# The last output tile in two column halves, each with its own bank, output tile, engine and queue

One core of one Trainium2 chip. The metric is the device time of one execution in microseconds (us), median of several. All runs told here are fast, with a granted TensorE clock of 0.997 to 1.0. The experiments ran in batches on several chips, each beside the kernel before.

In the views PE is TensorE, DVE VectorE, ACT ScalarE and SP SyncE; a q behind the name is the engine's queue. PSUM is the memory into which TensorE writes its sums, in banks. A semaphore is a counter that instructions wait for. A transfer's landing is its arrival; the profile gives the time from issue to landing. Of each view only the lines that matter are shown, and code and diffs are shortened.

## The reference

Linformer attention over 8 batches and 8 heads, then a dense layer with a hard-swish. The change touches only the last product, `g @ w_out`, and of its 64 output tiles of 128 tokens by 512 columns only the last.

```python
k_proj = einsum('ks,bhsd->bhkd', E, k); v_proj = einsum('ks,bhsd->bhkd', F, v)
attn = softmax(q @ k_proj^T / sqrt(64)); x = (attn @ v_proj) as [8192 tokens, 512]
h = x @ w_in                       # [8192, 2048]
g = h * clip(h + 3, 0, 6) / 6
out = g @ w_out                    # [8192, 512], float32
```

## The kernel before

The order of instructions on each engine is the order of the program. `pmm()` gives a bank of PSUM (128 x 512 float32) from a ring of four, `opool` an output tile from a ring of four. For the last tile the program already had a branch: two half copies on two engines and two transfers on two queues, but one bank and one output tile.

```python
opool = ctx.enter_context(tc.tile_pool(name="o", bufs=4))
ps_mm = ctx.enter_context(tc.tile_pool(name="ps_mm", bufs=4, space=bass.MemoryType.PSUM))
def pmm():
    return ps_mm.tile([P, TOK], f32, tag="mm", name="mm")
# ... cut ...
def second_group(b, t, g, c, copy=None):
    o_ps = pmm()
    for fo in range(FO):                      # 16 matmuls of 512 columns
        nc.tensor.matmul(o_ps, g[:, fo, c * P:(c + 1) * P], w_out_sb[:, fo, :],
                         start=(fo == 0), stop=(fo == FO - 1))
        if fo % SB == SB - 1:
            yield
    o_sb = opool.tile([P, d_model], f32, tag="o_sb", name="o_sb")
    o_dst = out_rows(b, t, c)
    if (b, t, c) == (B - 1, NB - 1, SB - 1):
        half = slice(0, d_model // 2), slice(d_model // 2, d_model)
        nc.vector.tensor_copy(o_sb[:, half[0]], o_ps[:, half[0]])
        nc.scalar.copy(o_sb[:, half[1]], o_ps[:, half[1]])
        nc.sync.dma_start(out=o_dst[:, half[0]], in_=o_sb[:, half[0]])
        nc.scalar.dma_start(out=o_dst[:, half[1]], in_=o_sb[:, half[1]])
        return
    (copy or nc.scalar.copy)(o_sb, o_ps)
    nc.sync.dma_start(out=o_dst, in_=o_sb)
# ... cut ...
for c in range(SB):                           # the last four tiles, nothing beside them
    whole(second_group(*behind[0], c))
```

The softmax here doesn't subtract the row's maximum and nothing guards it: scores larger than these inputs give would overflow.

## Time and profile before

| | before |
|---|---|
| median of the first 3 runs | 511.65 us (511.52 to 511.9) |
| span of the profiled run, which took 511.81 us | 510.0 us |
| TensorE busy | 98% |
| last matmul ends, by the chain | 505.91 us |
| last transfer issued | 506.85 us |

The page gives each engine's busy time and the chain of work that ended last; the timeline gives start, length, engine, line and what ended the idle time before it. TensorE bounds the body. The change concerns the 4.1 us between its last matmul and the end. This is the closing line of the program, L613, on SP's queue in the stretch of the tail: count, lengths in ns, first and last start.

```profile
L613 SPq EVENT_SEMAPHORE  x11: 17/28/28, 506.8 to 510.0; - x11
L613 SPq DRAIN  x3: 7/7/13, 509.2 to 509.5; - x3
```

SP waits for semaphores one after another, drains for the first time at 509.2, and the closing barrier runs to 510.0. The last transfer landed at about 506.85 + 1.8 = 508.65, so some 0.55 us lie between that and the first drain.

### The profile page before, as it was taken

The page shows a single profiled execution, that of the slowest core. Times are in us where ns is not written, and L with a number is a line of the kernel's source. Part 1 is how long each engine was busy: PE and PEld are TensorE (multiplying, and loading weights), DVE is VectorE, ACT ScalarE, POOL GpSimd, SP SyncE. Part 2 cuts the span into 40 slices and gives each one's busy share as a digit, 9 for nine tenths or more (in the row PEclk, how much of TensorE's full clock was granted, in tenths as well). Part 3 has the DMA queues.
Part 4 walks back from the last instruction along what each step waited for, and adds up shares of the span by engine and source line. Part 5 has one row for each costly group of instructions (what it writes and reads, how often), then busy time and mean ns, then how long its engine had stood idle before and what let it go on. Part 6 is the DMA issues. An engine that isn't in the chain of part 4 may idle for free.

```text
span 510.0 us, 7106 instructions
## 1 busy us (share of the span) xinstructions
PE 497.4 (98%) x2750; PEld 224.3 (44%) x2802; DVE 257.5 (50%) x401; ACT 274.5 (54%) x493; POOL 37.9 (7%) x57
## 2 busy tenths in 40 slices
PE   8899999999899999999999999999999999999996
PEld 3444444444344444444444444444444444444442
DVE  3572735855655733656434743467444563334420
ACT  3657476567576545664466644674447654444431
POOL 8610020010100200002000020000000000000000
PEclk9999999999999999999999999999999999999999
DMA  9999999599299493516924188421110111101112
GB/s 165 199 205 207 202 156 236 97 159 176 88 184 186 91 218 76 125 41 91 225 57 94 52 141 169 107 58 33 42 41 25 38 42 42 42 21 42 41 51 74
DMA packets 74210, 55.39 MB, mean 109 GB/s; under 512 B 35520, under 2 KB 65984, under 8 KB 74176
## 3 DMA queue, kind: packets, MB, share of 16 engines
q0 software_dynamic: 31952, 29.36, 37.0%
q1 hardware_dynamic: 42000, 25.17, 19.4%
q10 hardware_dynamic: 224, 0.39, 0.3%
q8 instruction: 22, 0.36, 0.3%
q14 instruction: 12, 0.10, 0.1%
HBM read 59.24 MB, written 16.78 MB: 149 GB/s over the span
## 4 chain that ended last, share of the span: by engine, by line
PE 94%; DMA 3%; issue 1%; POOL 1%; DVE 0%; ACT 0%; DVEq 0%; POOLq 0%
PE mm L470 43%; PE mm L450 43%; PE at L181 3%; DMA w_in_sb<-in_moe_w_in_dram 2%; PE at L227 1%; PE mm L227 1%; DMA k<-in_k_dram 1%; PE at L209 1%; PE mm L209 0%; PE at L370 0%; POOL q L97 0%; DVE kp L187 0%; POOL k L101 0%; PE at L350 0%; DVE xT L246 0%
## 5 line engine op out<-in xcount | busy, mean ns | idle before, releaser
L456 DVE SCALAR_TENSOR_TENSOR g<-r,mm 128x512 bf16<-128x512 f32 x256 | 173.8, 686 | 131.8 <-ACT r L455 130.4
L470 PE MATMUL mm<-w_out_sb,g 128*128 128x512 bf16 x995 | 231.8, 379 | 1.7 <-issue 0.5
L450 PE MATMUL mm<-xT,w_in_sb 128*128 128x512 bf16 x1001 | 229.2, 379 | 3.1 <-DVE xT L246 1.2
L455 ACT ACTIVATE r<-mm 128x512 f32<-128x512 f32 x256 | 152.8, 599 | 76.2 <-PE mm L450 73.7
L450 PEld LDWEIGHTS <-w_in_sb 128*128 128x128 bf16 x1024 | 99.4, 98 | 124.0 <-issue 5.5
L470 PEld LDWEIGHTS <-g 128*128 128x128 bf16 x1024 | 98.0, 98 | 121.5 <-issue 7.2
L484 ACT COPY o_sb<-mm 128x512 f32<-128x512 f32 x35 | 20.3, 587 | 91.5 <-PE mm L470 91.5
L484 DVE COPY o_sb<-mm 128x512 f32<-128x512 f32 x28 | 19.3, 691 | 67.3 <-PE mm L470 64.2
L159 ACT ACTIVATE rec<-mm 128x512 f32<-128x512 f32 x34 | 19.0, 595 | 34.1 <-PE mm L227 17.6
L163 ACT ACTIVATE rec<-rec 128x512 f32<-128x512 f32 x60 | 35.6, 637 | 0.0
L246 DVE TENSOR_TENSOR xT<-at,rec 128x512 bf16<-128x512 f32 x44 | 28.1, 680 | 7.1 <-ACT rec L163 7.1
L218 ACT ACTIVATE aT<-at 128x512 bf16<-128x512 f32 x44 | 23.1, 613 | 0.9 <-PE at L209 0.9
L159 ACT ACTIVATE rec<-at 128x512 f32<-128x512 f32 x30 | 17.3, 598 | 6.0 <-PE at L227 3.7
L199 POOL COPY mark<-kT 1x1 bf16<-1x1 bf16 x5 | 0.9, 178 | 210.1 <-DMA kT<-kp 210.1
L181 PE MATMUL at<-k,e_t 128*64 128x512 bf16 x56 | 13.4, 382 | 0.0
L181 PE MATMUL at<-v,f_t 128*64 128x512 bf16 x56 | 13.4, 382 | 0.0
L187 DVE CAST kp<-at 64x512 bf16<-64x512 f32 x14 | 9.0, 678 | 4.9 <-PE at L181 4.9
L218 ACT ACTIVATE aT<-mm 128x512 bf16<-128x512 f32 x12 | 6.5, 594 | 8.9 <-PE mm L209 8.9
L190 DVE CAST vp<-at 64x512 bf16<-64x512 f32 x14 | 9.7, 694 | 0.4
L181 PEld LDWEIGHTS <-e_t 128*64 128x64 bf16 x56 | 5.6, 109 | 7.2 <-PE at L227 2.1
L479 DVE COPY o_sb<-mm 128x256 f32<-128x256 f32 x1 | 0.4, 425 | 16.0 <-PE mm L470 16.0
L227 PE MATMUL at<-aT,vp 64*64 64x512 bf16 x88 | 8.5, 376 | 0.0
(62 smaller groups left out, 147.0 us busy)
## 6 DMA issues: line engine op xcount, KB each, us to landing
out_dram<-o_sb SPq DMA_DIRECT2D x63, 256.0 KB, 2.0
k<-in_k_dram POOLq DMA_DIRECT2D x7, 1024.0 KB, 15.4
v<-in_v_dram POOLq DMA_DIRECT2D x7, 1024.0 KB, 21.0
q<-in_q_dram POOLq DMA_DIRECT2D x7, 1024.0 KB, 10.5
w_out_sb<-in_moe_w_out_dram POOLq DMA_DIRECT2D x4, 512.0 KB, 17.1
k<-in_k_dram POOLq DMA_DIRECT2D x4, 256.0 KB, 5.8
v<-in_v_dram POOLq DMA_DIRECT2D x4, 256.0 KB, 7.9
w_in_sb<-in_moe_w_in_dram POOLq DMA_DIRECT2D x2, 512.0 KB, 11.9
```

The costliest lines, as they stand in the source:

```text
L159: nc.scalar.activation(ln, den, AF.Ln)
L163: nc.scalar.activation(ln, ln, AF.Exp, scale=-1.0)
L181: nc.tensor.matmul(ps[e * KP:(e + 1) * KP], ef_t[e][:, so, :], kqv[self.b]["kv"[e]][:, :, so, :], start=(so == 0), stop=(so == SO - 1))
L190: nc.vector.tensor_copy(self.vp[a * KP:(a + 1) * KP], self.ps[KP:].rearrange("p (h d) -> p h d", d=D))
L218: nc.scalar.activation(self.aT[j][:, r].rearrange("p a n -> p (a n)"), tiles[r], AF.Exp, scale=scale)
L227: nc.tensor.matmul(tiles[t][c:c + D].rearrange("p (r n) -> p r n", r=2), stationary(r, 2 * j + a), self.aT[j][r:r + KP, :, a, :], start=Tr ...
L246: nc.vector.tensor_mul(self.xT[:, j, t, :], av[t], recs[t])
L450: nc.tensor.matmul(h_ps, w_in_sb[:, ko, fo * P:(fo + 1) * P], xT[:, ko, t, :], start=(ko == 0), stop=(ko == KO - 1))
L455: nc.scalar.activation(r, h_ps, AF.Relu, bias=0.5, scale=1.0 / 6.0)
L456: nc.vector.scalar_tensor_tensor(g[:, fo, :], r, 1.0, h_ps, op0=ALU.min, op1=ALU.mult)
L470: nc.tensor.matmul(o_ps, g[:, fo, c * P:(c + 1) * P], w_out_sb[:, fo, :], start=(fo == 0), stop=(fo == FO - 1))
L484: (copy or nc.scalar.copy)(o_sb, o_ps)
```

## The change

The intent: the left half finishes while TensorE still works on the right one, and its copy and transfer are gone from behind the last matmul.

```diff
 def second_group(b, t, g, c, copy=None):
+    o_dst = out_rows(b, t, c)
+    if (b, t, c) == (B - 1, NB - 1, SB - 1):
+        for e, copy, dma in ((0, nc.vector.tensor_copy, nc.sync), (1, nc.scalar.copy, nc.scalar)):
+            half = slice(e * d_model // 2, (e + 1) * d_model // 2)
+            o_ps = pmm()[:, :d_model // 2]
+            for fo in range(FO):
+                nc.tensor.matmul(o_ps, g[:, fo, c * P:(c + 1) * P], w_out_sb[:, fo, half],
+                                 start=(fo == 0), stop=(fo == FO - 1))
+            o_sb = opool.tile([P, d_model], f32, tag="o_sb", name="o_sb")[:, :d_model // 2]
+            copy(o_sb, o_ps)
+            dma.dma_start(out=o_dst[:, half], in_=o_sb)
+        return
     o_ps = pmm()
     # ... 16 matmuls of 512 columns, unchanged ...
-    if (b, t, c) == (B - 1, NB - 1, SB - 1):
-        ... two half copies out of one bank, two transfers ...
-        return
```

More of the change, by code (lines that the diff above doesn't have):

```diff
@@ L474, in second_group @@
         o_sb = opool.tile([P, d_model], f32, tag="o_sb", name="o_sb")
-        o_dst = out_rows(b, t, c)
-        if (b, t, c) == (B - 1, NB - 1, SB - 1):
-            half = slice(0, d_model // 2), slice(d_model // 2, d_model)
-            nc.vector.tensor_copy(o_sb[:, half[0]], o_ps[:, half[0]])
-            nc.scalar.copy(o_sb[:, half[1]], o_ps[:, half[1]])
-            nc.sync.dma_start(out=o_dst[:, half[0]], in_=o_sb[:, half[0]])
-            nc.scalar.dma_start(out=o_dst[:, half[1]], in_=o_sb[:, half[1]])
-            return
         (copy or nc.scalar.copy)(o_sb, o_ps)
```

## The prediction

> **What bounds the kernel now.** I read the page first, by engine and by line, to see what sets the length of the whole.
>
> ```profile
> PE 497.4 (98%) x2750; PEld 224.3 (44%) x2802; DVE 257.5 (50%) x401; ACT 274.5 (54%) x493; POOL 37.9 (7%) x57
> PE 94%; DMA 3%; issue 1%; POOL 1%; DVE 0%; ACT 0%; DVEq 0%; POOLq 0%
> L470 PE MATMUL mm<-w_out_sb,g 128*128 128x512 bf16 x995 | 231.8, 379 | 1.7 <-issue 0.5
> ```
>
> TensorE is busy in 98% of the span and holds 94% of the chain that ended last; line 470, the second product, is one of its two large groups. The change does not touch that body. It touches the last of 64 output tiles, so the question is what stands behind the last matmul. For that I read the chain of waits over the last 20 us and then the timeline of the last seven, in order of time (start, length, what).
>
> ```profile
> 497.10 8.81 PE mm L470 x40
> 505.91 0.04 DVEq L479
> 505.94 0.04 issue
> 505.98 0.44 DVE o_sb L479
> 506.42 0.02 issue
> 506.44 0.37 ACT o_sb L480
> ```
>
> ```profile
> 502.52 0.59 ACT L484 COPY o_sb<-mm 128x512 f32<-128x512 f32 x1 [2.91 <-PE mm L470]
> ...
> 505.98 0.42 DVE L479 COPY o_sb<-mm 128x256 f32<-128x256 f32 x1 [16.00 <-PE mm L470]
> 506.44 0.33 SPq L481 DMA_DIRECT2D out_dram<-o_sb  x1
> 506.44 0.37 ACT L480 COPY o_sb<-mm 128x256 f32<-128x256 f32 x1 [3.34 <-DVE o_sb L479]
> 506.85 0.36 ACTq L482 DMA_DIRECT2D out_dram<-o_sb  x1
> ```
>
> The reader is to see two things. The two half copies were written to run side by side, on two engines, but they run one after the other: ScalarE's copy is released by VectorE's ("<-DVE o_sb L479"), not by TensorE, because both read one bank. And the last transfer is issued at 506.85, 0.94 us after the last matmul ended at 505.91. What follows is fixed: that transfer lands 1.8 us after its issue (the page of DMA issues in the window), at about 508.65, the SP queue's own waits show it waiting 1.9 us for it, and the closing semaphores run to 510.0, another 1.35 us. The sum 505.91 + 0.94 + 1.8 + 1.35 is the span of 510.0; 511.65 is the measured time, 1.65 us more for a start and end that the span leaves out, and which I take as unchanged.
>
> **What the Trainium skill says.** (1) "PSUM — Partial Sum Buffer", section "PSUM bank collisions raise a hardware error": no two engines may access one bank in the same partitions at once, two reads of disjoint columns included, and a dependency has to keep them apart. The trace agrees: the 0.46 us from 505.98 to 506.44 are that dependency. Two banks need none. (2) "TensorE: Matmul & The Clock Gate", section "Back-to-back issue gap": N columns take N / 2.4 + 2.5 ns in a stream, but with a weight load to each matmul 128 columns sustain only some 81 ns. The trace agrees with the first and not with the second, worked out below (56 ns with loads). (3) "DMA: Bandwidth & Descriptors", section "Issuing engines are not separate DMA queues": transfers of two queues share the same 16 DMA engines and interleave. In the trace, q1 (SP) fills 507.3 to 507.7 and q10 (ACT) 507.7 to 508.2, with 10 SP packets left among the first 53 ACT packets: they hardly meet. (4) The same page, section "Anatomy of one DMA", gives a fixed cost of about 2 us, mostly the receipt of the write. Here 128 KB land after 1.8 us and 256 KB after 2.0 us, so a half-size transfer saves little and cannot be hidden when it is the last.
>
> **The change, part by part.**
>
> *Matmuls.* Removed: 16 matmuls of 512 columns with 16 weight loads. Added: 32 of 256 columns, each with its own load of 128x128, first all of the left half, then all of the right. Cost of the old: the same copy or its like after each of the last groups starts at 492.12 (ACT) and 505.98 (DVE), so four groups take 13.86 us, one 3.465 us, one matmul 216.6 ns. There is no 128x128 by 256 matmul with loads in this trace, so I go between two points. At 128 columns the transposes of line 350 have a 128x128 load each:
>
> ```profile
> 33.90 0.61 PE L350 MATMUL at<-ident,q 128*128 128x128 bf16 x8
> 15.94 0.62 PE L338 MATMUL at<-v,f_t 128*128 128x128 bf16 x8
> ```
>
> Eight take 0.61 us, of which the last one's record is 219 ns: (610 - 219) / 7 = 56 ns from start to start. Line 338, real matmuls with a load each, gives 57 in the same way. So a load whose record is 98 ns does not hold up even a 56 ns stream; it holds up a 109 ns one less. Straight line: 56 + (216.6 - 56) x 128 / 384 = 109.5 ns; the skill's formula gives 109.2. New cost: 32 x 109.5 = 3.504 us, or **+0.04 us**, all on the path. The tail of the last matmul behind its issue, 379 - 217 = 162 ns for 512 columns and 270 - 109 = 161 for the 64x64 tiles of 256 columns (line 209, 270 ns), is the same.
>
> *Left half.* Its 16 matmuls end half a group (1.75 us) before the end, at about 504.2; the VectorE copy (0.42 us, as now) and SP's transfer then run beside the right half's matmuls: issued about 504.7, landed about 506.5, before the last packets move. **Taken off the path: the whole VectorE copy and the step to ScalarE**, 506.44 - 505.98 = 0.46 us.
>
> *Right half.* ScalarE waits for TensorE alone. It starts as long after the last matmul as VectorE did: the 502.52 copy of ScalarE plus one group of 3.465 is 505.98, just where VectorE started. With the +0.04 it starts at 506.02, takes 0.37 as now, and its transfer is issued 0.04 later, as now: 506.43 in place of 506.85. **Net: -0.42 us**. Landing (1.8) and closing (1.35) follow unchanged: span 509.6 us.
>
> *Buffers.* One more of four banks and one more of four output tiles are taken. The fifth output tile of the last five reuses the one whose transfer was issued at 492.73 and landed 2.0 us later, over 11 us before; its bank was emptied by 492.7. Both are free long before, so no new wait.
>
> Sum: 511.65 - 0.42 = **511.23 us**, 0.08% faster.
>
> **The rivals.** *Loads become the bound.* If a load and a matmul did not overlap, 98 + 107 = 205 ns each would make 32 x 205 = 6.56 us, 3.1 us longer: 511.65 + 3.1 - 0.46 = 514.3. Lines 338 and 350 speak against it. The skill's sustained 81 ns in place of 56 at 128 columns, carried over as 25 ns a matmul, would add 32 x 25 = 0.8 us: about 512.0, slower by 0.07%. *The gain is hidden or eaten.* If the end hung on something other than the ACT transfer, or a longer issue, a fetch of the new instructions (gaps named "issue" of 0.05 us stand in the chain) or a wait for a slot took it, the time would stay at 511.65. For it: only the smallness of the gain against the spread of the three runs, 0.38 us. Against it: nothing else is in flight after 508.2. *More than the sum.* If the ACT transfer is now held up by SP's packets, alone it could land up to 0.2 us sooner: 511.0. The packets overlap little, so I give it little.
>
> **Range and chances.** Centre 511.2. The low end takes the third rival and half the spread, 510.9; the high end takes a gain all but lost, or a chip that runs a little slower, 511.6. A change of 2% is 10 us, and the whole tail behind the last matmul is 4.1 us, so "within 2%" is all but certain; even the worst rival is 0.5%.
>
> **What the changed profile would show.** Right: the matmul groups of 256 columns at about 109 ns start to start, 3.5 us for 32; a VectorE copy near 504.3 and an SP transfer near 504.7, both before the last matmul; the ScalarE copy near 506.0, released by TensorE ("<-PE mm"); the ACT transfer near 506.4, landing in 1.8 us or a trifle less; the span near 509.6. Wrong: more than 3.6 us for the 32 matmuls; a ScalarE copy still released by VectorE or by a DMA; or a span unchanged though that transfer was issued earlier. A time off by several tenths with this tail as told would mean drift in the body of the kernel, which the change does not touch.

## The result

| | before | after |
|---|---|---|
| median, 6 runs each | 511.50 us (511.27 to 511.9) | 511.06 us (511.0 to 511.49) |
| ratio, 95% interval | | 0.9992 (0.9979 to 1.0005) |
| span of the profiled run | 510.0 us | 509.7 us |

A ratio is the mean time of one kernel's fast runs over that of the other's in the same rounds, so not quite the ratio of the medians. By the interval the times alone do not even show the sign. The traces do. First the timeline of the last seven us of the changed kernel, then its chain of waits over the last 9 us.

```profile
502.41 3.66 PE L475 MATMUL mm<-w_out_sb,g 128*128 128x256 bf16 x32
502.65 0.58 ACT L488 COPY o_sb<-mm 128x512 f32<-128x512 f32 x1 [2.91 <-PE mm L483]
...
504.41 0.42 DVE L478 COPY o_sb<-mm 128x256 f32<-128x256 f32 x1 [14.30 <-PE mm L475]
504.86 0.33 SPq L479 DMA_DIRECT2D out_dram<-o_sb  x1
506.14 0.37 ACT L478 COPY o_sb<-mm 128x256 f32<-128x256 f32 x1 [2.91 <-PE mm L475]
506.55 0.35 ACTq L479 DMA_DIRECT2D out_dram<-o_sb  x1
```

```profile
502.57 3.51 PE mm L475 x32
506.08 0.03 ACTq L478
506.10 0.04 issue
506.14 0.37 ACT o_sb L478
```

The VectorE step has gone from the chain: ScalarE's copy is released by TensorE ("<-PE mm L475"). The VectorE copy and SP's transfer lie 1.7 us ahead, beside the right half's matmuls. The chain gives the 32 matmuls 3.51 us; in the trace they start 109.2 ns apart.

The absolute times need care. The changed kernel reached the tail 0.13 us later (the ScalarE copy of the last whole tile starts at 502.65, before at 502.52), and that part of the program is the same in both. I therefore measure from that copy, the **anchor**, in every trace. Over the traces the anchor itself falls anywhere between 501.92 and 502.65, a wider spread than the whole effect.

| from the anchor, us | before | after | difference |
|---|---|---|---|
| to the last copy's start | 3.92 | 3.49 | -0.43 |
| to the last transfer's issue | 4.33 | 3.90 | -0.43 |
| to the end of the span | 7.48 | 7.05 | -0.43 |

Spans are given to 0.1 us, so the last row is good to about that.

### The profile page after: what moved, and what is told of

It reads as the page before. It is cut to its first block, busy times and chain, and to the rows that moved or that the text cites. A ratio compares the mean times of both kernels' runs of the same rounds, so it can differ in the third digit from the quotient of the medians.

```text
span 509.7 us, 7138 instructions
## 1 busy us (share of the span) xinstructions
PE 497.3 (98%) x2766; PEld 225.8 (44%) x2818; DVE 257.7 (51%) x401; ACT 274.4 (54%) x493; POOL 37.9 (7%) x57
## 4 chain that ended last, share of the span: by engine, by line
PE 94%; DMA 3%; issue 1%; POOL 1%; DVE 0%; ACT 0%; ACTq 0%; POOLq 0%
PE mm L450 43%; PE mm L483 43%; PE at L181 3%; DMA w_in_sb<-in_moe_w_in_dram 2%; PE at L227 1%; PE mm L227 1%; DMA k<-in_k_dram 1%; PE at L209 1%; PE mm L475 1%; PE mm L209 0%; PE at L370 0%; POOL q L97 0%; DVE kp L187 0%; POOL k L101 0%; PE at L350 0%
## 5 line engine op out<-in xcount | busy, mean ns | idle before, releaser
L483 PE MATMUL mm<-w_out_sb,g 128*128 128x512 bf16 x979 | 228.4, 379 | 1.7 <-issue 0.5
L483 PEld LDWEIGHTS <-g 128*128 128x128 bf16 x1008 | 96.4, 98 | 119.6 <-issue 7.2
L84 PE MATMUL mm<-ones 128*128 128x512 bf16 x18 | 6.6, 493 | 1.5 <-DVE ones L77 1.5
```

## The experiments

In each, the anchor gives the measure. All results are correct; all times are medians of 4 to 6 runs. Each diff is against the changed kernel, except where the kernel before is named. The interval of the ratio leaves out 1 only for the moved rotation in the changed kernel and for the two kernels with 384 and 128 columns, so the causes are read from the traces.

### Two banks, both halves to the end together

```diff
-for e: for fo: matmul(o_ps[e], ...); copy; dma
+for fo: for e: matmul(o_ps[e], ...)
+for e: copy; dma
```

> Two banks as in the change, but both halves advance together, so both end with the last matmul. I measure from the start of ScalarE's copy of the third-last... that is the last whole tile (before: 502.52, after: 502.65) to the end of the span: 7.48 us before, 7.05 after. Theory (the separate banks give the gain, and the early left half keeps the two transfers apart): both copies run side by side, ScalarE's released by TensorE, but two 128 KB transfers are issued within 0.1 us and share the DMA engines, so the last lands 0.2 to 0.4 us later: 7.25 to 7.45. Rival 1 (banks alone give it, transfers don't matter): 7.05. Rival 2 (the gain needs the left copy early, not the banks): 7.48.

```profile
505.38 0.42 DVE L479 COPY o_sb<-mm 128x256 f32<-128x256 f32 x1 [15.93 <-PE mm L475]
505.48 0.37 ACT L479 COPY o_sb<-mm 128x256 f32<-128x256 f32 x1 [2.91 <-PE mm L475]
505.83 0.33 SPq L480 DMA_DIRECT2D out_dram<-o_sb  x1
505.88 0.36 ACTq L480 DMA_DIRECT2D out_dram<-o_sb  x1
```

These lines are the timeline of this run (anchor 501.99). Two copies out of two banks run at once, at the same length as alone. So the wait is gone without an early left half: last issue 3.89 us behind the anchor, as in the change. Landing was slower, as my theory had it: SP's half landed 1.9 us after its issue and ScalarE's 2.1, 0.3 more than the change's 1.8. But the span ended 7.11 behind the anchor (median 510.97), not at 7.25 to 7.45. The size of my expectation failed: 0.3 us of later landing cost 0.06, which is within the rounding of the spans. Something between landing and end had given time back.

### One bank, two output tiles, two engines, two queues

```diff
+o_both = pmm()
 for e, copy, dma in ...:
-    o_ps = pmm()[:, :d_model // 2]
+    o_ps = o_both[:, half]
```

> The change with both halves in one bank; all else as in it. Theory (the bank is the dependency): the right half's matmuls wait for VectorE's copy of the left half, so TensorE stands still for its drain, start and copy, 0.16 + 0.08 + 0.42 and a step back, some 0.7 us: 7.75 us from the last whole tile's copy to the end, slower than before (7.48). Rival (the output tiles and queues give the gain, not the bank): 7.05, as in the change.

The chain of waits of this run, start, length, what (anchor 502.44):

```profile
502.35 1.76 PE mm L476 x16
504.12 0.03 DVEq L479
504.15 0.04 issue
504.19 0.43 DVE o_sb L479
504.63 0.04 issue
504.67 1.92 PE mm L476 x16
```

TensorE stands still until VectorE has read the bank, its second half waits 0.57 us and takes 1.92 us in the chain in place of 1.76, as its first matmul no longer starts while the one before it still runs (in the timeline both halves take 1.91). The last issue (507.06) comes 4.62 us behind the anchor, the end 7.76; expected was 7.75. Median 511.87 against 511.47 before. The bank is the dependency, as the order of the program and its semaphores make it.

The wait is TensorE's for VectorE here, and ScalarE's for VectorE in the kernel before. That one has a rival which no run takes alone: its two copies also wrote one output tile. Two builds that were not run on the chip speak for the bank. With one bank and two output tiles, ScalarE's last copy still waits for VectorE's semaphore; with the interleaved kernel's two banks and one output tile it does not.

### The bank alone: one engine, one output tile, one queue

```diff
+o_one = opool.tile([P, d_model], f32, tag="o_sb", name="o_sb")
-for e, copy, dma in ((0, nc.vector.tensor_copy, nc.sync), (1, nc.scalar.copy, nc.scalar)):
+for e, copy, dma in ((0, nc.scalar.copy, nc.sync), (1, nc.scalar.copy, nc.sync)):
     o_ps = pmm()[:, :d_model // 2]
-    o_sb = opool.tile(...)[:, :d_model // 2]
+    o_sb = o_one[:, half]
```

> The change with its two banks alone: ScalarE makes both copies, into one output tile, and SP issues both transfers; the semaphore of the last one is the first of the 8, as in the change. Theory (the bank and the early left half are all that matters; engine, tile and queue are free, as the left half is done 1.7 us earlier): 3.90 us from the last whole tile's copy to the last issue and 7.05 to 7.1 to the end of the span. Rival (the second engine or queue matters): a wait shows ahead of the last copy or issue, 7.2 us or more.

```profile
503.73 0.37 ACT L479 COPY o_sb<-mm 128x256 f32<-128x256 f32 x1 [1.16 <-PE mm L476]
504.12 2.04 SPq L480 DMA_DIRECT2D out_dram<-o_sb  x2
505.43 0.37 ACT L479 COPY o_sb<-mm 128x256 f32<-128x256 f32 x1 [1.33 <-PE mm L476]
```

Both copies are released by TensorE. Anchor 501.98, last copy at 505.43 (3.45), last issue at 505.83 (3.85, where 3.90 was expected), span 509.0: 7.02 to the end, median 510.91. The second engine, output tile and queue of the change add no measurable gain.

### The plain tile

```diff
-# the whole branch for the last tile
+# one bank, 16 matmuls of 512 columns, one ScalarE copy, one SP transfer of 256 KB
```

> The last tile handled like every other: one bank, 16 matmuls of 512 columns, one ScalarE copy, one SP transfer of 256 KB. Theory (the old split gained next to nothing, as its copies ran one after the other): the copy takes 0.59 in place of 0.46 + 0.37, the transfer 2.0 in place of 1.8, so 3.45 + 0.59 + 0.04 + 2.0 + 1.35 = 7.43 us from the last whole tile's copy to the end, the kernel before (7.48) within 0.1. Rival (the old split was worth something): above 7.6.

```profile
502.30 0.59 ACT L486 COPY o_sb<-mm 128x512 f32<-128x512 f32 x1 [2.91 <-PE mm L481]
...
505.75 0.59 ACT L476 COPY o_sb<-mm 128x512 f32<-128x512 f32 x1 [2.87 <-PE mm L473]
506.36 0.33 SPq L477 DMA_DIRECT2D out_dram<-o_sb  x1
```

Last issue 4.06 us behind the anchor and 2.0 us to landing, as expected (508.36), but the span ended at 509.3, 7.00 behind the anchor, and not 7.43: **as short as the change, without any of it** (median 510.91). This was the miss that mattered. The closing lines of SP's queue show where the 0.4 us are. Of the changed kernel (landing at 506.55 + 1.8 = 508.35), from 508.3 to 509:

```profile
L617 SPq EVENT_SEMAPHORE  x8: 28/28/28, 508.4 to 508.8; - x8
L617 SPq DRAIN  x2: 7/10/13, 508.9 to 508.9; - x2
```

Of the plain one (landing at 508.36), from 508.2 to 508.5:

```profile
L615 SPq EVENT_SEMAPHORE  x1: 28/28/28, 508.4 to 508.4; - x1
L615 SPq DRAIN  x1: 13/13/13, 508.4 to 508.4; - x1
```

In the change SP still went through eight waits, some 0.06 us from one to the next, before it drained; in the plain kernel one, as it had passed the others by 507.2. The framework gives the transfers of SP and ScalarE eight semaphores in rotation, and SP's closing list waits for them in the order 0 to 7. The kernel before and the change have 81 such transfers, so the last one is on number 0 and all the others are still to be gone through when it lands. The plain tile has 80; its last one is on number 7. In the interleaved kernel the framework had put ScalarE's transfer ahead of SP's in the rotation, so ScalarE's later landing was on number 7 and SP's earlier one (505.83 + 1.9 = 507.73) on number 0. This is SP's closing list there, from 507.7 to 508.27:

```profile
L618 SPq EVENT_SEMAPHORE  x8: 27/28/28, 507.8 to 508.2; - x8
L618 SPq DRAIN  x1: 13/13/13, 508.2 to 508.2; - x1
```

Four of the eight waits start before ScalarE's landing at about 507.98, and number 7 comes only after it. So the list, started by the earlier landing, led to the end, and the later one cost next to nothing. That explains that miss too.

### Only the rotation moved

To test this, one whole-tile store, some 40 us ahead of the end, goes to GpSimd's queue, which has semaphores of its own. This leaves 80 in the rotation. The tail is untouched.

```diff
-    nc.sync.dma_start(out=o_dst, in_=o_sb)
+    (nc.gpsimd if (b, t, c) == (B - 1, 0, 0) else nc.sync).dma_start(out=o_dst, in_=o_sb)
```

In the changed kernel:

> The change, with one whole output tile of the last batch's first half (some 40 us before the end) stored through GpSimd's queue. Nothing else differs; but the program hands 8 semaphores round to the transfers of SP and ScalarE in turn, and so the last transfer gets the last of the 8 in the closing order of waits, where the change's has the first. Theory (behind the landing, SP still goes through the waits that come after that semaphore, 7 or 8 steps of some 0.06 us): last landing as before, first drain of SP within 0.1 us of it in place of 0.55, 6.6 us from the last whole tile's copy to the end, some 510.6 us. Rival (the closing is fixed, and the whole-tile store was shorter there because it used one queue): 7.05 us, 511.05.

```profile
L617 SPq EVENT_SEMAPHORE  x1: 28/28/28, 508.0 to 508.0; - x1
L617 SPq DRAIN  x2: 7/10/13, 508.0 to 508.1; - x2
```

These are its closing lines from 507.85 to 508.1: one wait, then the drain. (The records of seven earlier waits are missing from this trace; that of the kernel before with the same move, below, has them all.) The tail to the last issue is the change's (anchor 502.23, issue 506.13, 3.90), landing at 507.93, first drain at 508.0, end at 508.9: 6.67 us behind the anchor, 510.64 us median, ratio 0.9981 (0.9968 to 0.9993). In the kernel before, with the same edit:

> The kernel before, with the same one whole-tile store moved to GpSimd's queue, so that its last transfer too gets the last of the 8 semaphores. Theory (the place in the closing order is worth 0.45 us whatever the last tile looks like, and the change's own gain is 0.43): 4.33 us from the last whole tile's copy to the last issue, as before, and 7.03 to the end in place of 7.48; some 511.05 us. Rival (the move of the store gains in some other way in the change's kernel): 7.48 to the end.

Anchor 502.15, last issue at 506.47 (4.32), landing 508.27, first drain 508.4, end 509.2: 7.05, median 511.08. And the other way round, the plain tile with one transfer more in the rotation, by cutting the store ahead of it in two:

```diff
+if (b, t, c) == (B - 1, NB - 1, SB - 2):
+    for half in (left, right): nc.sync.dma_start(out=o_dst[:, half], in_=o_sb[:, half])
```

> The plain last tile, with the store of the tile before it cut in two halves on SP, 3 us ahead of the last and off the path; this moves the last transfer from the last of the 8 semaphores to the first. Theory (place in the closing order of waits): 7.45 us from the last whole tile's copy to the end in place of 7.00, some 511.4 us, as the kernel before. Rival (one queue at the end is what makes it short): 7.00, some 510.9.

```profile
L619 SPq EVENT_SEMAPHORE  x8: 27/28/28, 508.0 to 508.4; - x8
L619 SPq DRAIN  x2: 7/10/13, 508.5 to 508.6; - x2
```

These are its closing lines from 507.9 to 508.6. Anchor 501.93, last issue 505.99, landing 507.99; the eight waits are back, end 509.3: 7.37, median 511.36. All three fit; the rivals (a fixed closing, a gain by the moved store itself, or one queue being shorter) don't. With the semaphore equal, the change is ahead of the plain tile after all: 7.05 against 7.37 us on number 0, 6.67 against 7.00 on number 7.

The change itself was run again beside these as a control:

> The change itself once more, as the control of this batch: 7.05 us from the last whole tile's copy to the end of the span, ScalarE's transfer issued 3.90 us after that copy, SP's closing waits 0.5 us long behind the last landing; some 511.05 us.

It gave 502.41 to 506.31 (3.90) and 509.5 (7.09), with the first drain at 508.6, 0.5 behind the landing, median 511.24 against 511.53 before in the same rounds, ratio 0.9992 (0.9978 to 1.0005).

### Uneven pieces

```diff
-halves of 256 and 256 columns
+pieces of 384 and 128 columns
```

> The change with pieces of 384 and 128 columns. Theory (what is left behind the last matmul is the last copy and its transfer, and both shrink with the piece): ScalarE's copy 0.27 in place of 0.37, the transfer of 64 KB 0.1 to 0.2 sooner, TensorE as before: 6.75 to 6.95 us from the last whole tile's copy to the end, 0.1 to 0.3 us less than the change. Rival (fixed costs rule, the small piece loses in its short rows what it saves): 7.0 to 7.1.

Anchor 501.92, last issue 505.71 (3.79), landing 1.6 us later, end 508.7 (6.78), median 510.62, ratio 0.9983 (0.997 to 0.9997). TensorE took as long as with halves: the last copy starts 3.49 behind the anchor in both. Combined with the moved rotation:

> Pieces of 384 and 128 columns, and the last transfer on the last semaphore, by the same move of one store. Theory (the two gains are independent): 6.78 - 0.45 = 6.35 us from the last whole tile's copy to the end, some 510.2 us. Rival (with the small piece the earlier transfer of 192 KB, which lands only 0.3 us sooner, then holds the end): 6.5 or more.

Anchor 502.55, end 508.8: 6.25, median 510.51 (510.0 to 510.64), ratio 0.9975 (0.9963 to 0.9988). The rival's 6.5 or more did not come. This is the fastest kernel by median, and the ends by the anchor add up: 7.05 - 0.27 for the piece and - 0.4 to 0.5 for the rotation. Then the cut was pushed on, to find the loads:

> Pieces of 448 and 64 columns, last transfer on the last semaphore, against 384 and 128 (3.79 us to the last issue, 6.25 to the end). This asks the rival of the prediction where it could hold: 64 columns would stream in 29 ns, less than the 56 ns at which loads have been seen to keep up. If loads don't bound: 16 x 190 + 16 x 29 = 3.50 us of TensorE as before, copy 0.2 in place of 0.27: 3.72 to the last issue, 6.2 to the end. If they bound at some 56 ns: TensorE 0.4 us longer, 4.1 to the last issue, 6.6 to the end. Its transfer has rows of 256 bytes, which may cost some tenths besides.

The groups of this run's last 9 us, busy us and mean ns:

```profile
L475 PE MATMUL mm<-w_out_sb,g 128*128 128x448 bf16 x16 | 3.2, 352 | 0.0
L475 PEld LDWEIGHTS <-g 128*128 128x128 bf16 x32 | 2.2, 98 | 1.7
L475 PE MATMUL mm<-w_out_sb,g 128*128 128x64 bf16 x16 | 0.6, 193 | 0.0
```

Loads did not bound even here: in the trace the 16 matmuls of 64 columns with a load each start 29 ns apart, and the last copy starts 3.50 us behind the anchor (with halves 3.49). The last issue came at 505.96, 3.74 behind the anchor (502.22). But the end came at 509.1, 6.9, and not 6.2: the left piece now finishes so late that its transfer is issued at 505.91, 0.05 us ahead of the other, and the two took 2.1 and 2.2 us to land. The short rows of the small one may have a part in that; no run separates them. Median 510.9.

## Why the prediction was right

- **What bounds the tail.** Confirmed. With two banks and the early left half, but one engine, output tile and queue, the gain is there; with all else of it and one bank it turns into a loss.
- **Matmuls, +0.04 us.** Predicted 109.5 ns each and 3.504 us; measured 109.2 from start to start, and 3.51 us by the chain. From the anchor to the copy after the last group, 3.49 us against 3.46 of VectorE's start before: +0.03.
- **Left half off the path, -0.46; net -0.42.** Measured -0.43 to the last copy, to the last issue and to the end. With the anchor's 0.13 taken off, the VectorE copy, SP's issue, ScalarE's copy and its issue were at 504.28, 504.73, 506.01 and 506.42; the text has 504.3, 504.7, 506.0 and 506.4.
- **Time.** Predicted 511.23, measured 511.06 and, in the control, 511.24. Measured gains by medians of the same rounds are 0.44 and 0.29 us, against 0.42. The body's drift, which the text named, is of the same size: the median of the kernel before alone went from 511.65 to 511.50 with three more runs. So it is partly luck that the absolute time fell this near. Both intervals of the ratio include 1; the gain is shown by the traces, not by the times.
- **Rivals.** Loads as the bound: wrong down to 64 columns. Gain hidden: wrong. A sooner landing of the ScalarE transfer: wrong for the change, 1.8 us in both; landing was slower only in the two kernels whose last transfers were issued 0.05 us apart (interleaved and 448/64), against 0.41 before.
- **The weak step.** "What follows is fixed" held for this change only because both programs have 81 transfers in the rotation, which the prediction did not look at: luck. The 1.35 us of closing are some 0.5 of waits gone through after the landing and 0.8 of barrier, and the first part hangs on a count that nobody chose. Had the change removed one such transfer, the sum would have been off by its own size. It also hid that the old branch for the last tile was no gain over the plain tile: 4.33 against 4.06 us to the last issue, and 7.48 to the end against 7.37 with the same semaphore, 7.05 against 7.00 with the other.
- **Small slips that cost nothing.** The 1.65 us outside the span set the median of three runs against the span of another run: the profiled one took 511.81, so it is 1.8 (after: 511.49 - 509.7, the same). It drops out of the difference. In the buffer step the tile issued at 492.73 is the left half's; the right half takes the next, whose transfer landed at about 498.2, 7.8 us ahead. No wait for either shows.

What stays open: why the body drifts by some tenths from run to run, and whether the landing of the 448/64 kernel is slowed by the meeting of the transfers or by the short rows.

## What to carry to other kernels

Where one engine ends the kernel, list what stands behind its last instruction and shrink that: a last piece in a bank of its own, small, with the rest done beside the work ahead of it, but not too small: 448 and 64 columns ended at 6.9 us behind the anchor, 384 and 128 at 6.25. Check the closing too: the place of the last transfer's semaphore in the closing list of waits was worth as much here (0.4 to 0.5 us) as the whole rewrite of the last tile. When an effect is smaller than the spread of the times, measure it in the traces from an anchor that the change does not touch.

## What the Trainium skill lacked or had wrong

- "TensorE: Matmul & The Clock Gate", "Back-to-back issue gap": its sustained figures with weight loads, about 81 ns at 128 columns and 131 ns at 512, are not seen. With a 128x128 load to each matmul these traces have 29 ns at 64 columns, 56 at 128, 109.2 at 256 and 216.6 at 512, which is what its formula for a single, isolated matmul gives (N / 2.4 + 2.5).
- The same page, "LDWEIGHTS (loading the stationary operand)": columns / 1.2 gives 107 ns for a load of 128 columns. The record is 98 ns long, and loads follow at 29 ns without holding up the matmuls. The page also describes a faster load path; no run here shows whether it was in use.
- "DMA: Bandwidth & Descriptors", "Anatomy of one DMA": its 2.0 us + bytes / 436e3 is fitted to GpSimd's path, and the page has no such sum for stores from SP and ScalarE. Here they landed 1.6 us (64 KB), 1.7 to 1.8 (128 KB) and 2.0 (256 KB) after the issue began, where two were not issued together.
- No page has the closing waits: these programs end by going through one semaphore after another at some 0.06 us each, and the last transfer's place in that list moved the end by 0.4 to 0.5 us.
